# Moving casts, fills and early loads at the hand-over from the projections to attention

## The chip, the cores and the metric

The kernel runs on one core of a Trainium2 chip. The metric is the device time of one execution in microseconds; the median of three runs of the kernel before is 1693.15 us (1690.56 to 1694.89).

The engines are named as in the profile: PE is the matrix engine (TensorE; PEld its weight loads), DVE is VectorE, ACT is ScalarE, POOL is GpSimd, and SP is the queue from which this kernel issues its DMAs. Each engine works through its own instructions in order and waits for others by semaphores.

## The reference

One transformer block with adaptive layer norm: attention over 2048 positions with 32 heads of 16, then a dense layer, Mish, and a dense layer.

```python
S, D, F, H, Dh = 2048, 512, 1792, 32, 16
sa, ca, ga, sb, cb, gb = split(silu(c) @ w_mod)          # six rows of 512
h = layernorm(x) * (1 + ca) + sa
q, k, v = heads(h @ wqkv)                                # (32, 2048, 16) each
x = x + ga * (merge(softmax(q @ k.T * Dh**-0.5) @ v) @ wo)
h = layernorm(x) * (1 + cb) + sb
x = x + gb * (mish(h @ w1 + b1) @ w2)
```

All of it is fp32. The kernel forms a product of two fp32 matrices from rounded parts: each operand is split into a rounded value (hi, type fp32r) and the rest (lo), and three products hi·hi, hi·lo and lo·hi are summed.

## The kernel before

**Projections.** The first part (`lp` pool) loads x, normalizes it, transposes it in four blocks of 512 positions (`tr_tb`) into `h_h` and `h_l` (hi and lo), and projects. A weight slice of 128 columns (`wr`) is loaded by `slice_load` and split by `slice_split`: `hi_copy` writes `wh` on ScalarE (line 88), `lo_sub` writes `wl` on GpSimd (line 95). `qk_unit` projects queries or keys of eight heads for one block of 512 positions into one PSUM bank; its `fin` takes them out of PSUM, splits them into `qh` and `ql`, and writes them to a scratch in DRAM (`qscr`, `kscr`). There are two ways out: without a time `h`, ScalarE casts `qh` straight from PSUM and VectorE subtracts `ql`, which reads the bank too; with a time, ScalarE copies the bank to `qf` and GpSimd makes both parts of it. `v_unit` projects values, which ScalarE copies to `vq` (line 299). In this first part the loop over the four blocks `tb` does the keys of heads 0 to 7, one query unit, and some value units, and loads each finished block of keys back from scratch into `ka` (`load_k`, line 330), laid out for the scores.

**Banks.** PSUM has a ring of six banks (`ring`) and two banks of their own, `ms` and `acc`. Until the scores start, two of the six serve other units, so maxima turn round in four.

**Row maxima.** Softmax needs the row maxima first. The steps t = -20 to -1 (`PRO`) compute scores for maxima only: `max_pair` (lines 595 and 597) runs two matmuls side by side into two ring banks, and one VectorE reduce of 128x1024 takes both. 32 pairs make up the maxima of the first four heads, in four key blocks of eight pairs; eight pairs of the next four heads follow (they read `ka2` and `qa2`). `neg_max` and `max_rows` bring the maxima into `mt`, and DMAs put them into rows of `qa` (line 625). Between two pairs `dense_slots` puts matmuls of further projection units (`plan`, `planned`, line 133): the query slice 1, values, the key slices 1 and 2, and so on. From step 0 on each step computes scores (line 636), their exponentials on ScalarE (line 639), the product with the values (line 654) and, beside them, the maxima of later heads (lines 581 and 583) and the remaining dense work.

**Order.** The program's order is written out by hand: `at(h, f)` puts a function into the list of half step h, and `run_hooks(h)` runs it as the program is recorded; two half steps make a step, and h = -40 is the first. `planned` gives the loads and splits of later slices their half steps when a unit of an earlier slice ends.

**Early preparations.** Six blocks of w1 are split before the main part: `early_prep` loads a block (`ep`, line 1570), GpSimd splits it seven half steps later, and three half steps after that two DMAs write it to `w1scr` (line 1578). The tiles `ka2` to `ka4` are filled with ones on GpSimd (line 561) before rows of keys are loaded over them; `load_pair(2)` at h = -22 loads `qa2` and `ka2`, `load_pair(3)` at h = -10 the next.

Of the kernel before, what the change touches and what calls it, by code (L numbers as in the profile page):

```python
# [8 lines left out]
F32 = mybir.dt.float32  # L9
# [9 lines left out]
def adaln_block(ctx: ExitStack, tc: tile.TileContext, x, wqkv, wo, w1, b1, w2, c, w_mod, out):  # L19
    nc = tc.nc  # L20
# [8 lines left out]
    NB = S // TB  # L29
# [9 lines left out]
    PRO = 16 + LEAD  # L39
# [4 lines left out]
    LATE_LOAD = {4: -4, 5: 9}  # L44
# [41 lines left out]
    def hi_copy(eng, hi, src):  # L86
        if eng == "a":
            nc.scalar.copy(hi, src)
        elif eng == "v":
            nc.vector.tensor_copy(hi, src)  # L90
        else:
            nc.gpsimd.tensor_scalar(hi, src, 1.0, 0.0, op0=ALU.mult, op1=ALU.add)
# [110 lines left out]
    def at(h, f):  # L203

        hooks.setdefault(h, []).append(f)
# [23 lines left out]
    def slice_load(kind, i, pool=None, lp=None):  # L229
        w = P if kind < 2 else 2 * P  # L230
        raw = (pool or qp).tile([P, DK, w], F32, tag="raw" if pool is pw else "wr", name="wr", bufs=2 if lp else 1)
        o = kind * D + i * w
        nc.sync.dma_start(raw, wqkv[:, o:o + w].rearrange("(k p) m -> p k m", p=P))
        slices[kind, i] = raw

    def slice_split(kind, i, pool=None, eng="p", hi_eng="a"):
        raw = slices[kind, i]
        w = raw.shape[2]
        hi = (pool or qp).tile([P, DK, w], F32R, tag="wh", name="wh", bufs=2)
        lo = (pool or qp).tile([P, DK, w], F32R, tag="wl", name="wl", bufs=2)  # L240
        hi_copy(hi_eng, hi, raw)
        lo_sub(eng, lo, raw, hi)
        slices[kind, i] = (hi, lo)

    def qk_unit(kind, ct, tb, tag):

        wh, wl = slices[kind, ct]
        acc = bank(tag)
        ts_ = slice(tb * TB, (tb + 1) * TB)
        mm3(acc, [wh[:, k, :] for k in range(DK)], [wl[:, k, :] for k in range(DK)],  # L250
            [h_h[:, k, ts_] for k in range(DK)], [h_l[:, k, ts_] for k in range(DK)], "b")

        def fin(h=None):
            late = h is not None and -4 <= h < 3
            if late and not spares:
                for v in range(2):
                    both = ap.tile([P, DK, TB], F32R, tag=f"o_{v}", name="late", bufs=1)
                    spares.extend(both[:, i, :] for i in range(DK))
            if late:
                qh, ql = spares.pop(), spares.pop()  # L260
            else:
                qh = qp.tile([P, TB], F32R, tag="qh", name="qh", bufs=2)
                ql = qp.tile([P, TB], F32R, tag="ql", name="ql", bufs=2)
            if h is None:
                hi_copy("a", qh, acc)
                lo_sub("v", ql, acc, qh)
            else:
                qf = (ap.tile([P, TB], F32, tag=f"p{len(spares) // 2 % 2 * 2}", name="qf", bufs=3) if late else
                      pw.tile([P, TB], F32, tag="raw", name="qf", bufs=1))
                nc.scalar.copy(qf, acc)  # L270
                hi_copy("p", qh, qf)
                lo_sub("p", ql, qf, qh)
            scr, rows = (qscr, 50) if kind == 0 else (kscr, 48)

            def put():
                put_away.add((kind, ct, tb))
                o = 8 * ct * rows * S + tb * TB
                if kind == 0:
                    for r, src in enumerate((qh, qh, ql)):
                        nc.sync.dma_start(dap(scr, o + r * S, [[rows * S, 8], [3 * S, DH], [1, TB]]), src.bitcast(F32))  # L280
                    return
                hi = qh.bitcast(F32)
                twice = bass.AP(tensor=hi.tensor, offset=hi.offset, ap=[list(hi.ap)[0], [0, 2], [1, TB]])
                nc.sync.dma_start(dap(scr, o, [[3 * S, P], [2 * S, 2], [1, TB]]), twice)
                nc.sync.dma_start(dap(scr, o + S, [[3 * S, P], [1, TB]]), ql.bitcast(F32))

            put() if h is None else at(clear(h + (5 if h > 60 else 2)), put)
        return fin
# [34 lines left out]
    def load_k(pp, tb=None):  # L323
        n, j = divmod(pp, 2)
        h = 4 * (n % G) + 2 * j
        kt = ka[pp % NR].bitcast(F32)
        at_ = slice(0, S) if tb is None else slice(tb * TB, (tb + 1) * TB)
        assert {(1, h // 8, i) for i in (range(NB) if tb is None else (tb,))} <= put_away, (pp, put_away)
        for s in range(2):
            nc.sync.dma_start(kt[64 * s:64 * s + 48, at_], kscr[h + s, :, at_])  # L330
# [6 lines left out]
    with ExitStack() as es:  # L337
# [65 lines left out]
        def apply_tb(tb):  # L403
            rs = rss.pop(tb)
            for i in range(4):
                xt = xts[4 * tb + i]
                nc.scalar.activation(xt, xt, AF.Identity, scale=rs[:, 1, i:i + 1], bias=rs[:, 2, i:i + 1])
# [115 lines left out]
        for tb in range(NB):  # L523
            if tb + 2 < NB:
                stats_tb(tb + 2)
            parts = []
            early = []
            for kind in (1, 0) if tb == 0 else (1,):
                fin = qk_unit(kind, 0, tb, "ring")
                parts.append((pe_queue[2 * DK:], fin))  # L530
                early.append(pe_queue[:2 * DK])
                pe_queue.clear()
            if tb == 0:
                (kw, qw) = early
                early = [[m for k in range(DK) for m in (kw[k], qw[k], kw[DK + k])], qw[DK:]]
            pe_queue.extend(m for e in early for m in e)
            pe_run()
            if tb in (1, 2):
                for kc in (2 * tb - 2, 2 * tb - 1):
                    unit(v_unit(0, kc, "ring"))  # L540
            if tb + 1 < NB:
                tr_tb(tb + 1, CUT1)
            for late, fin in parts:
                pe_queue.extend(late)
                unit(fin)
            if tb + 1 < NB:
                tr_tb(tb + 1, CUT2)
            if tb + 2 < NB:
                apply_tb(tb + 2)
            if tb == 0:  # L550
                for pp in range(2):
                    load_q(pp, 48)
            for pp in range(2):
                load_k(pp, tb)
        slice_split(0, 1)


    kq2 = ctx.enter_context(tc.tile_pool(name="kq2", bufs=1))
    ka += [kq2.tile([P, S], F32R, name=f"ka{i}") for i in range(2, NR)]
    for t in ka[2:]:  # L560
        nc.gpsimd.memset(t.bitcast(F32), 1.0)
    ap = ctx.enter_context(tc.tile_pool(name="ap", bufs=1, reuse_waits="tile"))
    vgs = {}

# [527 lines left out]
    _, w1s, w2s, wos = state[last]  # L1092
# [419 lines left out]
    def planned(i, a, tag):  # L1512
        _, kind, sl, args = plan[i]
        unit = v_unit(sl, a, tag) if kind == 2 else qk_unit(kind, sl, a, tag)

        def fin(h):
            if a == args[-1]:
                if i + 2 < len(plan):
                    d = 4 if h > 0 else 1
                    split_at[i + 2] = LATE_SPLIT.get(i + 2, h + d)  # L1520
                    split = lambda: slice_split(*plan[i + 2][1:3], hi_eng="p" if h > 0 else "a")
                    split() if h < -4 else at(split_at[i + 2], split)
                if i + 3 < len(plan):
                    at(LATE_LOAD.get(i + 3, h + 7), lambda: slice_load(*plan[i + 3][1:3]))
            unit(h)
            if (kind, sl, a) == (2, 0, NKC - 1):
                at(max(0, h + 2), lambda: first_mods(max(0, h + 2)))
            if i + 1 == len(plan) and a == args[-1]:
                mst["qkv"] = h // 2 + 3
        return fin  # L1530

    at(-2 * PRO, lambda: slice_load(*plan[2][1:3]))
    order = (3, 4, 2, 5)

    def first_mods(h, j=0):
# [26 lines left out]

    EARLY = 6

    def early_prep(i, h):

        scr, src, _ = preps[i]
        lo, hi = [ap.tile([P, TB], F32R, tag=f"p{(1, 3, 0, 2)[i % 4]}", name="ep", bufs=4 - i % 4 // 2) for _ in range(2)]
        raw = lo.bitcast(F32)
        nc.sync.dma_start(raw.rearrange("p (k m) -> p k m", m=P), src)  # L1570

        def split():
            hi_copy("p", hi, raw)
            lo_sub("p", lo, raw, hi)

        def put():
            for v, part in enumerate((hi, lo)):
                nc.sync.dma_start(scr[:, v, :], part.bitcast(F32))

        at(h + 7, split)  # L1580
        at(h + 10, put)

    for i in range(EARLY):
        at(3 * i - 37, lambda i=i: early_prep(i, 3 * i - 37))

    def start_preps(h, i=EARLY, turn=0, puts=()):

# [75 lines left out]
```

## Time and profile before

| what | value |
|---|---|
| median of three runs | 1693.15 us (1690.56 to 1694.89) |
| profiled execution, its own time | 1691.93 us |
| span of its instructions | 1690.1 us |
| granted TensorE clock, mean | 0.996 |
| PE busy | 1667.0 us, 99% of the span |
| DVE, ACT, POOL busy | 85%, 80%, 48% |
| DMA moved | 239.02 MB, mean 141 GB/s |

In the rows that follow in the prediction, the first number is the start in us from the start of the span and the second the duration. Then come the engine, the source line, the operation, what it writes and reads (`out<-in`, the program's own names), the shape and a count of such instructions. A bracket at the end gives the idle time of the engine just before, and what ended it. SPq marks DMAs issued by the SP queue; the duration is that of the issue, not of the transfer.

### The profile page before, as it was taken

The numbers are of one execution on the slowest core, as the hardware profiler recorded it, in microseconds if no ns is written. First come the engines' busy times: TensorE is split into PE (matmuls) and PEld (weight loads), VectorE is DVE, ScalarE is ACT, GpSimd is POOL, SyncE is SP. The second block draws the span as 40 slices with busy tenths as digits, with TensorE's granted clock in tenths as the row PEclk, the third lists the DMA queues.
The fourth block names the chain that finished last, engine by engine and source line by source line (L and its number), as shares of the span: only waits on it lengthen the run. The fifth ranks groups of instructions, "written<-read, shape, count | busy, mean of one in ns | idle before, by whom it ended". The sixth has DMA issues, their size and how long they took to land.

```text
span 1690.1 us, 34360 instructions
## 1 busy us (share of the span) xinstructions
PE 1667.0 (99%) x12707; PEld 932.1 (55%) x12707; DVE 1431.6 (85%) x2372; ACT 1357.3 (80%) x2618; POOL 812.5 (48%) x839
## 2 busy tenths in 40 slices
PE   8989999999999999999999999999999999999999
PEld 6855665555444455555555455555555455555687
DVE  6978888888989888888889888888889888883377
ACT  7157777777778988888888998888888998889674
POOL 5556224655313564556323565556323565555442
PEclk9999999999999999999999999999999999999999
DMA  7777556777755433434355434534354433534161
GB/s 261 218 272 200 147 147 188 222 222 216 230 146 143 113 95 93 121 88 129 85 137 152 115 77 93 141 76 126 87 145 122 130 94 81 144 103 131 76 228 63
DMA packets 114984, 239.02 MB, mean 141 GB/s; under 512 B 24500, under 2 KB 50120, under 8 KB 108864
## 3 DMA queue, kind: packets, MB, share of 16 engines
q1 hardware_dynamic: 114808, 236.82, 49.5%
q8 instruction: 100, 1.64, 0.4%
q14 instruction: 68, 0.56, 0.1%
q10 hardware_dynamic: 8, 0.00, 0.0%
HBM read 180.48 MB, written 51.45 MB: 137 GB/s over the span
## 4 chain that ended last, share of the span: by engine, by line
PE 89%; DVE 4%; DMA 3%; ACT 2%; issue 1%; SPq 0%; POOL 0%; ACTq 0%; DVEq 0%; POOLq 0%
PE bk L654 29%; PE ring L636 22%; PE ring L581 19%; PE bk L133 11%; PE ring L1267 2%; PE ring L126 2%; DVE mx L583 2%; ACT pr L639 1%; PE bk L126 1%; DVE mx L597 1%; PE ring L133 1%; DMA ka<-kscr 1%; DMA kscr<-qh 0%; DMA qa<-mt 0%; PE ring L970 0%
## 5 line engine op out<-in xcount | busy, mean ns | idle before, releaser
L583 DVE TENSOR_REDUCE mx<-ring 128x1 f32<-128x512 f32 x1968 | 1221.9, 681 | 151.1 <-PE ring L581 136.6
L639 ACT ACTIVATE pr<-ring 128x512 f32<-128x512 f32 x2048 | 1078.5, 603 | 207.5 <-PE bk L133 122.7
L581 PE MATMUL ring<-ka,qa 64*128 64x512 f32 x1968 | 817.8, 429 | 1.2 <-ACT pr L639 1.0
L636 PE MATMUL ring<-qa,ka 64*128 64x512 f32 x2048 | 759.1, 402 | 3.4 <-ACT pr L639 1.9
L654 PE MATMUL bk<-pr,vg 128*32 128x512 f32 x4096 | 545.1, 604 | 0.0
L581 PEld LDWEIGHTS ring<-ka,qa 64*128 64x128 f32 x1968 | 350.6, 184 | 326.2 <-DVE mx L583 251.4
L636 PEld LDWEIGHTS ring<-qa,ka 64*128 64x128 f32 x2048 | 373.8, 184 | 192.3 <-DVE mx L583 113.2
L133 PE MATMUL bk<-h,w 64*128 64x512 f32 (+1 forms) x1080 | 277.9, 390 | 0.0
L133 PE MATMUL bk<-w,a_h 64*128 64x512 f32 x632 | 211.1, 413 | 0.0
L133 PEld LDWEIGHTS bk<-h,w 64*128 64x128 f32 x1080 | 178.6, 185 | 10.0 <-ACT pr L639 1.5
L654 PEld LDWEIGHTS bk<-pr,vg 128*32 128x32 f32 x4096 | 81.3, 108 | 135.6 <-issue 126.4
L133 PE MATMUL bk<-w,a_l 64*128 64x512 f32 x316 | 124.3, 393 | 0.0
L133 PEld LDWEIGHTS bk<-w,a_h 64*128 64x128 f32 x632 | 106.8, 184 | 3.0 <-ACT hb L848 0.8
L1026 POOL TENSOR_TENSOR y<-yd,y 128x512 f32<-128x512 f32 x44 | 56.9, 1292 | 88.9 <-ACT yd L1025 79.5
L860 POOL TENSOR_SCALAR qq<-ee 128x512 f32<-128x512 f32 x25 | 15.5, 621 | 169.1 <-ACT ee L854 169.1
L876 POOL TENSOR_TENSOR qq<-qq,rr 128x512 f32<-128x512 f32 x42 | 54.2, 1289 | 85.7 <-ACT rr L870 85.7
L862 POOL TENSOR_TENSOR hb<-hb,ee 128x512 f32<-128x512 f32 x42 | 54.1, 1288 | 79.7 <-DVE ee L858 77.7
L133 PE MATMUL bk<-w,o_hl 64*128 64x512 f32 x288 | 79.3, 405 | 0.0
L95 POOL TENSOR_TENSOR a_l<-hb,a_h 128x512 fp32r<-128x512 f32 x53 | 73.1, 1379 | 4.4
L133 PE MATMUL bk<-h_h,wl 64*128 64x512 f32 x192 | 63.3, 426 | 0.3 <-ACT pr L639 0.3
L133 PEld LDWEIGHTS bk<-w,a_l 64*128 64x128 f32 x316 | 58.3, 185 | 3.1
L133 PE MATMUL bk<-h_h,wh 64*128 64x512 f32 x192 | 53.9, 413 | 5.1 <-ACT vq L299 4.8
(226 smaller groups left out, 1902.6 us busy)
## 6 DMA issues: line engine op xcount, KB each, us to landing
ka<-kscr SPq DMA_DIRECT2D x124, 384.0 KB
w<-w2scr SPq DMA_DIRECT2D x56, 512.0 KB
w<-w1scr SPq DMA_DIRECT2D x46, 512.0 KB
vg<-vscr SPq DMA_DIRECT2D x32, 552.0 KB
qa<-qscr SPq DMA_DIRECT2D x124, 100.0 KB
qscr<-qh SPq DMA_DIRECT2D x32, 256.0 KB
w2scr<-hl SPq DMA_DIRECT2D x14, 512.0 KB
kscr<-qh SPq DMA_DIRECT2D x12, 512.0 KB
```

The costliest lines, as they stand in the source:

```text
L95: (nc.gpsimd if eng == "p" else nc.vector).tensor_sub(lo, src, hi.bitcast(F32))
L126: nc.tensor.matmul(acc, l, r, start=start, stop=stop)
L133: i = nc.tensor.matmul(acc, l[64 * g:64 * g + 64], r[64 * g:64 * g + 64], start=start and not then, stop=bool(stop and then))
L581: nc.tensor.matmul(pm, qt[64 * s:64 * s + 64, qs * P:(qs + 1) * P], kt[64 * s:64 * s + 64, kb * TB:(kb + 1) * TB], start=True, stop=True)
L583: nc.vector.tensor_reduce(out=mxs[n][:, s, 4 * j + qs, kb:kb + 1], in_=pm, op=ALU.max, axis=AX.X)
L636: nc.tensor.matmul(p_, kt[64 * s:64 * s + 64, kc * P:(kc + 1) * P], qt[64 * s:64 * s + 64, :], start=True, stop=True)
L639: e = nc.scalar.activation(pr, p_, AF.Exp, scale=SCALE)
L654: nc.tensor.matmul(accs[n][32 * h:32 * h + 32, :], vgs[n][:, o:o + 32], pts.pop((t, h)), start=(kc == 0), stop=(kc == 15))
L862: (nc.vector if tail else nc.gpsimd).tensor_mul(hb, hb, ee)
L876: nc.gpsimd.tensor_mul(qq, qq, rr)
L1026: nc.gpsimd.tensor_add(y[i], yd, y[i])
L1267: nc.tensor.matmul(po[i // 2][:, i % 2, :], l[:, s], w[:, r, :], start=(f == 0 and j == 0), stop=(f == FT - 1 and j == 2))
```

## The change

The edits all lie in the hand-over.

- The keys of the last block (kind 1, tb 3) are projected into the bank `ms` instead of a ring bank, and leave it by the second way: ScalarE copies to `qf`, GpSimd makes `qh` and `ql`.
- The query slice 1 is split in the turn of block 2, not after the loop.
- The loop loads only the key blocks 0 and 1 back. The blocks 2 and 3 are loaded at h = -40, interleaved with the loads of all six early preparations, behind the load of key slice 1.
- The early preparations are split at h = -38, -36, -34, -32, -27 and -25 and written three half steps later.
- The load of key slice 2 is recorded two half steps after its trigger instead of seven.
- `ka2`, `ka3` and `ka4` are filled at h = -30, -22 and -18.

```diff
@@ qk_unit, fin @@
-            if h is None:
+            if h is None and (kind, tb) != (1, NB - 1):
                 hi_copy("a", qh, acc)
                 lo_sub("v", ql, acc, qh)
             else:
@@ the loop over tb @@
-                fin = qk_unit(kind, 0, tb, "ring")
+                fin = qk_unit(kind, 0, tb, "ring" if tb + 1 < NB else "ms")
...
             if tb + 2 < NB:
                 apply_tb(tb + 2)
+            elif tb + 1 < NB:
+                slice_split(0, 1)
...
             for pp in range(2):
-                load_k(pp, tb)
-        slice_split(0, 1)
+                if tb < 2:
+                    load_k(pp, tb)
...
-    for t in ka[2:]:
-        nc.gpsimd.memset(t.bitcast(F32), 1.0)
+    for i, h in ((2, -30), (3, -22), (4, -18)):
+        at(h, lambda t=ka[i]: nc.gpsimd.memset(t.bitcast(F32), 1.0))
@@ planned, fin @@
-                    at(LATE_LOAD.get(i + 3, h + 7), lambda: slice_load(*plan[i + 3][1:3]))
+                    at(h + 2 if h < -20 else LATE_LOAD.get(i + 3, h + 7), lambda: slice_load(*plan[i + 3][1:3]))
...
-    at(-2 * PRO, lambda: slice_load(*plan[2][1:3]))
+    def first_loads():
+        slice_load(*plan[2][1:3])
+        for i in range(EARLY):
+            early_load(i)
+            if i % 2:
+                for pp in range(2):
+                    if i < 4:
+                        load_k(pp, 2 + i // 2)
+
+    at(-2 * PRO, first_loads)
...
-        at(h + 7, split)
-        at(h + 10, put)
+        at(h, split)
+        at(h + 3, put)

     for i in range(EARLY):
-        at(3 * i - 37, lambda i=i: early_prep(i, 3 * i - 37))
+        early_prep(i, (-38, -36, -34, -32, -27, -25)[i])
```

What this does to the order on the queues: on SP, before the change, from the scratch writes of the third key block to the second load of weights behind the first (`wr`; `ka_98` and `ka_99` are the key tiles of the first heads, `ka_700` is ka2):

```order
L284 DMA kscr<-qh 128x2x512
L285 DMA kscr<-ql 128x512
L330 DMA ka_98<-kscr 48x512 x2
L330 DMA ka_99<-kscr 48x512 x2
...
L233 DMA wr<-in_A_wqkv 128x4x128
L1570 DMA ep<-in_B_w 128x4x128 x4
L1578 DMA w1scr<-ep 128x512 x2
L280 DMA qscr<-qh 8x16x512 x2
...
L330 DMA ka_700<-kscr 48x2048 x2
L1578 DMA w1scr<-ep 128x512 x2
L233 DMA wr<-in_A_wqkv 128x4x128
```

The same place on SP after the change (ka2 is `ka_695` here):

```order
L284 DMA kscr<-qh 128x2x512
L285 DMA kscr<-ql 128x512
...
L233 DMA wr<-in_A_wqkv 128x4x128
L1582 DMA ep<-in_B_w 128x4x128 x2
L330 DMA ka_98<-kscr 48x512 x2
...
L1595 DMA w1scr<-ep 128x512 x8
L233 DMA wr<-in_A_wqkv 128x4x128
L280 DMA qscr<-qh 8x16x512 x2
...
L330 DMA ka_695<-kscr 48x2048 x2
```

The key loads of the blocks 2 and 3 moved behind the first `wr` and `ep` loads, the second `wr` load moved ahead of the query scratch and of ka2, and eight `w1scr` writes stand ahead of it where six stood.

On GpSimd, before, from the last `wl` of the first part to the query unit:

```order
L95 TENSOR_TENSOR wl<-wr,wh 128x512
L561 MEMSET ka_700 128x2048
L561 MEMSET ka_701 128x2048
L561 MEMSET ka_702 128x2048
L92 TENSOR_SCALAR ep<-ep 128x512
L95 TENSOR_TENSOR ep<-ep 128x512
L95 TENSOR_TENSOR wl<-wr,wh 128x512
L92 TENSOR_SCALAR qh<-qf 128x512
```

And after, at the same place:

```order
L95 TENSOR_TENSOR wl<-wr,wh 128x512
L92 TENSOR_SCALAR qh<-qf 128x512
L95 TENSOR_TENSOR ql<-qf,qh 128x512
L92 TENSOR_SCALAR ep<-ep 128x512
...
L562 MEMSET ka_695 128x2048
L95 TENSOR_TENSOR wl<-wr,wh 128x512
L92 TENSOR_SCALAR qh<-qf 128x512
```

The last keys' pair came in, four early splits (eight rows, cut) and one fill stand ahead of the next `wl` where one split and three fills stood. On ScalarE the cast `wh` comes ahead of the last key unit and that unit's cast became the copy `qf<-bk`. VectorE lost one `ql`; TensorE's order is the same but for the bank of twelve matmuls.

More of the change, by code (lines that the diff above doesn't have):

```diff
@@ L1563, in adaln_block, with early_load @@
     EARLY = 6
-    def early_prep(i, h):
+    raws = {}
+    def early_load(i):
         scr, src, _ = preps[i]
@@ L1570, in early_prep @@
         nc.sync.dma_start(raw.rearrange("p (k m) -> p k m", m=P), src)
+        raws[i] = scr, raw, hi, lo
+    def early_prep(i, h):
         def split():
+            scr, raw, hi, lo = raws[i]
             hi_copy("p", hi, raw)
@@ L1576, in put @@
         def put():
+            scr, _, hi, lo = raws.pop(i)
             for v, part in enumerate((hi, lo)):
                 nc.sync.dma_start(scr[:, v, :], part.bitcast(F32))
-        at(h + 7, split)
-        at(h + 10, put)
+        at(h, split)
+        at(h + 3, put)
     for i in range(EARLY):
-        at(3 * i - 37, lambda i=i: early_prep(i, 3 * i - 37))
+        early_prep(i, (-38, -36, -34, -32, -27, -25)[i])
     def start_preps(h, i=EARLY, turn=0, puts=()):
```

## The prediction

> **What bounds the kernel now.** I read the page first, then the busy time by stage, then the engines in order of time around the two places where the stages show TensorE idle.
>
> ```profile
> span 1690.1 us, 34360 instructions
> PE 1667.0 (99%) x12707; PEld 932.1 (55%) x12707; DVE 1431.6 (85%) x2372; ACT 1357.3 (80%) x2618; POOL 812.5 (48%) x839
> ```
>
> TensorE is busy 1667.0 of 1690.1 us. So any gain must be sought in the 23 us in which it is not, or in stretches where it is busy at a lower clock. The view by stages shows these; the columns are the stretch, its length, busy us (and instructions) of PE, PEld, DVE, ACT and POOL, then the granted clock, the DMA share and GB/s.
>
> ```profile
> 1200.00:1600.00 400.00, 399.32 (x3021) 209.23 (x3019) 311.22 (x529) 338.94 (x659) 194.67 (x198) 1.00 0.40 112
> ...
> 11.33:14.74 3.41, 2.29 (x38) 1.22 (x37) 1.67 (x5) 1.67 (x2) 0.98 (x2) 1.00 1.10 369
> 18.15:21.57 3.42, 1.67 (x8) 0.83 (x6) 3.35 (x6) 3.33 (x5) 3.26 (x6) 1.00 1.05 387
> 21.57:24.98 3.41, 3.41 (x11) 2.93 (x12) 3.34 (x7) 1.93 (x3) 0.00 (x1) 0.50 1.07 312
> 45.46:48.87 3.41, 1.80 (x9) 0.96 (x9) 1.64 (x3) 1.10 (x2) 1.31 (x2) 1.00 0.82 284
> 48.87:52.29 3.42, 3.42 (x26) 3.42 (x24) 2.45 (x2) 0.00 (x0) 3.42 (x3) 0.50 0.55 203
> 83.01:86.42 3.41, 0.89 (x8) 0.46 (x4) 2.34 (x3) 0.00 (x0) 0.00 (x0) 1.00 1.01 291
> 86.42:89.83 3.41, 1.16 (x5) 0.87 (x7) 0.00 (x0) 1.38 (x3) 1.41 (x2) 0.50 1.07 395
> 89.83:93.25 3.42, 3.42 (x20) 2.67 (x18) 1.85 (x4) 0.16 (x1) 1.72 (x2) 0.50 1.10 391
> ```
>
> In the attention proper TensorE idles 0.7 us in 400: work behind the hand-over cannot shrink, only start earlier. Before it the stretches of 3.41 us are cut where the clock changes. Each one with TensorE busy 1.80 us or less (1.67, 1.80, 0.89, 1.16) is followed by one at clock 0.50; the one with 2.29 us was followed by full clock. The change touches two of these places.
>
> **The first place** is the hand-over from the last key unit to the first maxima.
>
> ```profile
> 45.12 1.04 POOL L479 TENSOR_TENSOR h_l<-hf,modc 128x512 fp32r<-128x512 f32 x1 [1.62 <-DVE hf L474]
> 46.22 0.78 PE L126 MATMUL ring<-h_l,wh 128*128 128x512 f32 x2 [0.16 <-POOL h_l L479]
> 47.08 0.58 ACT L88 CAST qh<-ring 128x512 fp32r<-128x512 f32 x1 [2.97 <-PE ring L126]
> 47.70 0.69 DVE L95 TENSOR_TENSOR ql<-ring,qh 128x512 fp32r<-128x512 f32 x1 [1.25 <-ACT qh L88]
> 48.44 0.58 PE L595 MATMUL ring<-ka,qa 64*128 64x512 f32 x2 [1.44 <-DVE ql L95]
> 49.06 1.23 DVE L597 TENSOR_REDUCE mx<-ring 128x2 f32<-128x1024 f32 x1 [0.67 <-PE ring L595]
> 52.46 32.89 DVE L597 TENSOR_REDUCE mx<-ring 128x2 f32<-128x1024 f32 x29 [0.47 <-PE ring L595]
> ```
>
> The first maxima wait 1.44 us for a ring bank that ql still reads; the next stretch then runs at half clock. From the third reduce on VectorE is the bound of this stage: 29 in 32.89 us, 1.134 us each, without a gap.
>
> **The second place** is a chain through three queues.
>
> ```profile
> 64.07 1.71 SPq L1578 DMA_DIRECT2D w1scr<-ep  x2
> 79.00 0.38 SPq L233 DMA_DIRECT2D wr<-in_A_wqkv  x1
> 80.25 0.37 ACT L299 COPY vq<-bk 128x256 f32<-128x256 f32 x1 [2.32 <-PE bk L133]
> 87.72 0.62 ACT L88 CAST wh<-wr 128x512 fp32r<-128x512 f32 x1 [7.10 <-DMA wr<-in_A_wqkv]
> 88.25 0.37 ACT L299 COPY vq<-bk 128x256 f32<-128x256 f32 x1
> 83.45 0.44 PE L595 MATMUL ring<-ka,qa 64*128 64x512 f32 x2
> 88.67 2.13 PE L133 MATMUL bk<-h_h,wh 64*128 64x512 f32 x6 [4.77 <-ACT vq L299]
> 91.26 1.23 DVE L597 TENSOR_REDUCE mx<-ring 128x2 f32<-128x1024 f32 x1 [5.91 <-PE ring L595]
> 92.97 2.42 DVE L597 TENSOR_REDUCE mx<-ring 128x2 f32<-128x1024 f32 x2
> 95.99 7.01 DVE L597 TENSOR_REDUCE mx<-ring 128x2 f32<-128x1024 f32 x6 [0.35 <-PE ring L595]
> ```
>
> The weights wr of the third key slice are issued at 79.00, late in SP's queue among w1scr writes, and land 8.7 us later; ScalarE's cast waits for them, the value copy that frees a bank stands behind the cast, and TensorE stands 4.77 us. Two half-clock stretches follow.
>
> **The change, part by part.**
>
> Own bank, and the last keys on GpSimd: the maxima no longer share a bank with the last key unit, so nothing holds them after the matmuls that end at 46.22 + 0.78 = 47.00. A ScalarE copy and a GpSimd pair replace ScalarE's cast and the 0.69 us on VectorE. The copy goes into the buffer that held the raw query weights, so it waits for their wl. That moves ahead on GpSimd to the end of h_l (45.12 + 1.04 = 46.16) and takes 1.28 (row below): 47.44. The copy, as long as the cast, ends at 48.1, the GpSimd pair at 50.1. TensorE waits for none of this before the bank's next use, four pairs of maxima later (some 51.5). Gain: the first reduce follows its matmul by 49.06 − 48.44 = 0.62, and the matmul can be issued behind the last of the key unit at 46.8, which puts the reduce at 47.4, 1.66 us sooner. The bounds are 1.44 (the wait alone) and 1.66; I take 1.66. The key unit itself must now wait until the transposes in its new bank have been read, but it waits longer for other halves of h_h and h_l: nothing.
>
> Clock: with the wait gone, 45.46:48.87 is busy 1.80 + 1.44 = 3.24 us, above 2.29, so the drop should not come. The third reduce stands 3.40 us behind the first; at 1.134 each it would be 2.27. Gain 1.13; bounds 0 and 1.13. By the Trainium skill (TensorE: Matmul & The Clock Gate, Part 1: The HAM clock gate) the clock is halved after an idle window of some 3.4 us and given back after a busy one; the window of 1.80 us busy was not idle, so the trace is stricter than the page here. By the page this drop has another cause and stays, and the sum below would be 7.6 instead of 8.7.
>
> Query weights sooner: the cast wh, 0.62 us, moves to 44.1 on ScalarE, which is idle from there to 47.08 (2.97 us by its row); it costs nothing.
>
> Weights and loads sooner, key tiles filled later. Rows that carry the prices:
>
> ```profile
> 48.26 1.28 POOL L95 TENSOR_TENSOR wl<-wr,wh 128x512 fp32r<-128x512 f32 x1 [2.10 <-ACT wh L88]
> 49.48 5.29 POOL L561 MEMSET ka<- 128x2048 f32 x3
> 59.07 0.43 SPq L233 DMA_DIRECT2D wr<-in_A_wqkv  x1
> 59.61 2.09 SPq L1570 DMA_DIRECT2D ep<-in_B_w  x4
> 63.42 0.63 POOL L92 TENSOR_SCALAR ep<-ep 128x512 fp32r<-128x512 f32 x1 [8.65 <-DMA ep<-in_B_w]
> 64.13 1.28 POOL L95 TENSOR_TENSOR ep<-ep 128x512 fp32r<-128x512 f32 x1
> 70.08 0.39 PE L133 MATMUL bk<-h_h,wl 64*128 64x512 f32 x1
> 95.71 2.86 SPq L625 DMA_DIRECT2D qa<-mt  x4
> 103.05 0.49 PE L636 MATMUL ring<-qa,ka 64*128 64x512 f32 x1 [0.43 <-DVE mx L597]
> 48.87:103.49 54.62, 48.77 (x517) 43.87 (x515) 46.59 (x43) 8.89 (x27) 26.96 (x26) 0.91 0.83 257
> ```
>
> On SP the last key unit's two scratch writes now stand ahead of the loads of the third and fourth key blocks, and wait for the GpSimd pair: issued by 50.2. Behind them come wr of the second slice, at 50.7, and the first ep load at about 51.2 (59.07 and 59.61 before), then the third key block at 52 and, between more ep loads, the fourth at 55 to 57. The 17th and 25th pair of maxima, 16 and 24 × 1.134 us after 47.4, need those blocks at 65 and 74: hidden. The first ep load took 3.8 us from its issue to the split that waits for it (59.61 to 63.42); 8.7 (the wr load above) is the other end. I take 3.8, the same transfer: 55.0. GpSimd then does four splits (63.42 to 65.41, 1.99 each), one memset (5.29/3 = 1.76) and the second slice's wl (1.28): 55.0 + 7.96 + 1.76 + 1.28 = 66.0. TensorE first needs this wl at 70.08, in the new time 67.3 (2.8 sooner, 1.66 + 1.13), so 1.3 us to spare; with 8.7 it is 3.6 us late. The third slice's wr follows on SP at once, behind eight w1scr writes that are all released by 63: issued at 66, landed between 69.8 and 74.7. ScalarE needs it behind the copy of 80.25, in the new time 80.25 + 0.37 − 2.8 = 77.8. So the waits of 7.10 and 4.77 us vanish, and what TensorE meets next is VectorE's pace. GpSimd rounds the query unit by 68.0; its scratch write and then the load of qa2 and ka2 take 3.8 to 8.7 us each and end at 75.6 to 85.4. The first maxima on them come at 84: 0 to 1.4 us late, and I take 0, since the share of the transfers falls when they start sooner. Two more splits and the other two memsets end on GpSimd at 68.0 + 3.98 + 3.52 = 75.5, before the third slice's wl (about 79).
>
> What this is worth: between the end of reduce 31 (52.46 + 32.89 = 85.35) and the 35th at 95.99 lie 10.64 us. Undisturbed there are three reduces (1.23 + 2.42 = 3.65), 0.48 us of small reduces (91.26 + 1.23 to 92.97) and 0.60 after (95.39 to 95.99): 4.73. Gain 5.9; bounds 4.77 (wait alone) to 5.9.
>
> Sum: 1.66 + 1.13 + 5.9 = 8.7 us. The scores would start at 103.05 − 8.7 = 94.3; the last qa<-mt, issued 2.86 us after 87, lands in time even at the 4.5 us that 98.57 to 103.05 allowed. Behind this the program is the same and TensorE-bound. The profiled execution took 1691.93, so 1683.2; it lies 1.2 under the median of three, 1693.15, so **1684.4 us**.
>
> **The rivals.**
>
> GpSimd late (0.10): the second slice's wl behind four splits and a memset comes at 70.9 if the first ep load needs 8.7 us. For: two writes of 512 and 256 KB stand ahead of it. Against: the transfers' share was 0.55 at 48.87:52.29. TensorE waits 3.6 us, perhaps with half a stretch of low clock, 1.7: 1688.0 to 1689.7.
>
> Clock drop stays (0.07): if the drop at 48.87 has another cause than the 1.44 us wait, the 1.13 us are not won: 8.7 − 1.13 = 7.6, 1685.5. Against it stand the four low stretches, each followed by 0.50. The Trainium skill's page on the clock gate, named above, speaks for this case.
>
> Transfers bound the stage (0.10): from 48.87 to 103.49 they were busy 0.83 of 54.62 us, 45.3 us of work, and the shorter stage has 45.9. If they cannot be packed beyond 0.83, the maxima's rows arrive as late as now: 1693, no change. Against: 391 to 395 GB/s were reached where 257 is the mean, and the work now starts some 8 us sooner.
>
> Slower (0.07): the third slice's wr stands behind the eight w1scr writes, which wait for GpSimd, and behind wl. If SP is held there, each microsecond of landing past 77.8 is one that ScalarE's cast, and through it TensorE, waits. The gain is used up at 77.8 + 8.7 = 86.5; at 91.6 the kernel is 5.1 us slower, 1698.2. For it: such a queue is what made the stall of now. Against: 91.6 is 17 us behind the later of my two landings, and no wait in the rows is so long.
>
> **How the numbers follow.** The forecast has 0.66, its own range 1682.5 to 1686.5 (wait and clock bounds on one side, about 1 us of small TensorE gaps at 100 to 110 on the other). Within 0.3% (5.1 us, about what this kernel's measurement tells from no change) lie the transfers' case and half of GpSimd late. Faster: 0.66 + 0.07 + 0.05 = 0.78; same 0.10 + 0.05 = 0.15; slower 0.07. The range takes in GpSimd late: 1681.5 to 1689.7.
>
> **What would show it.** First maxima within 0.3 us of the last key unit; clock 1.00 in every stretch from 45 on; the third slice's wr on SP near 66 and no TensorE wait above 1 us at 75 to 95; scores from 94.3. Wrong if TensorE waits for wl near 67, if the cast still waits for wr, or if scores begin after 98.

## The result and the profile after

| | before | changed |
|---|---|---|
| median | 1693.15 us, 11 runs (1690.56 to 1697.11) | 1687.92 us, 11 runs (1685.39 to 1691.74) |
| ratio to before | | 0.9972, interval 0.9962 to 0.9981 |
| span of the profiled execution | 1690.1 us | 1684.5 us |

The change wins 5.2 us by the medians and 5.6 us in the two profiled executions, where 8.7 were forecast. The interval lies clear of 1, and the time is inside the range. In a later group of runs (run 11 below) the changed kernel came out at 0.9960 (0.9947 to 0.9972).

VectorE in order of time, changed kernel, from the first maxima to the eight pairs on the keys of pair 2:

```profile
47.06 21.58 DVE L598 TENSOR_REDUCE mx<-ring 128x2 f32<-128x1024 f32 x19 [1.05 <-PE ring L596]
69.51 14.90 DVE L598 TENSOR_REDUCE mx<-ring 128x2 f32<-128x1024 f32 x13 [0.87 <-PE ring L596]
86.73 1.23 DVE L598 TENSOR_REDUCE mx<-ring 128x2 f32<-128x1024 f32 x1 [1.94 <-PE ring L596]
88.51 1.23 DVE L598 TENSOR_REDUCE mx<-ring 128x2 f32<-128x1024 f32 x1 [0.55 <-PE ring L596]
90.36 6.99 DVE L598 TENSOR_REDUCE mx<-ring 128x2 f32<-128x1024 f32 x6
```

The first reduce stands at 47.06 (49.06 before), and the third at 47.06 + 2 × 1.136 = 49.33 (52.46 before): the first place went as forecast. Of the 2.0 us, 0.44 are no part of the change, since GpSimd's last h_l already starts at 44.68 instead of 45.12 here. The 35th reduce comes at 90.36 instead of 95.99, where 87.3 was forecast. The two holes that cost the rest are the 0.87 us ahead of 69.51 and the stretch from 69.51 + 14.90 = 84.41 to 90.36.

TensorE's waits in the same stage, changed kernel:

```profile
68.06 0.50 PE L133 MATMUL bk<-h_h,wl 64*128 64x512 f32 x1 [0.82 <-POOL wl L95]
84.86 0.47 PE L596 MATMUL ring<-ka,qa 64*128 64x512 f32 x1 [1.43 <-DVE mm L611]
85.93 0.76 PE L596 MATMUL ring<-ka,qa 64*128 64x512 f32 x1 [0.60 <-DMA ka<-kscr]
97.41 0.50 PE L637 MATMUL ring<-qa,ka 64*128 64x512 f32 x1 [0.43 <-DVE mx L598]
```

The wait of 4.77 us behind ScalarE's value copy is gone. In its place TensorE waits for wl of the second slice and then for the keys of pair 2, twice, one half of `ka2` after the other. (The profile puts the first of these two waits down to a small reduce that came last by its semaphores. In another execution of the same kernel, run 11 below, both are put down to the load.) The scores start at 97.41, 5.64 us sooner, which is the whole gain: from there to the end it takes 1587.1 us in both executions (1684.5 − 97.41 and 1690.1 − 103.05).

ScalarE's cast of the third slice, GpSimd, and SP's queue, changed kernel:

```profile
78.44 0.62 ACT L88 CAST wh<-wr 128x512 fp32r<-128x512 f32 x1
```

```profile
57.15 0.63 POOL L92 TENSOR_SCALAR ep<-ep 128x512 fp32r<-128x512 f32 x1 [7.29 <-PE ring L596]
64.97 1.81 POOL L562 MEMSET ka<- 128x2048 f32 x1
66.74 1.27 POOL L95 TENSOR_TENSOR wl<-wr,wh 128x512 fp32r<-128x512 f32 x1
```

```profile
51.42 1.43 SPq L1582 DMA_DIRECT2D ep<-in_B_w  x2
...
68.03 0.38 SPq L233 DMA_DIRECT2D wr<-in_A_wqkv  x1
...
70.67 3.60 SPq L1595 DMA_DIRECT2D w1scr<-ep  x2
74.36 0.81 SPq L306 DMA_DIRECT2D vscr<-vq  x1
75.26 1.91 SPq L1595 DMA_DIRECT2D w1scr<-ep  x2
77.23 1.74 SPq L321 DMA_DIRECT2D qa<-qscr  x2
79.06 0.77 SPq L330 DMA_DIRECT2D ka<-kscr  x2
```

The chain that replaced the stall stands in these rows. The first w1 split starts at 57.15, so wl ends at 68.01. On SP the third slice's weights follow at 68.03 and are in time, but `ka2`, which needs none of this, stands behind four w1scr writes and a value write and is issued only at 79.06. TensorE's second product on it starts at 85.93, 6.9 us after.

The stage by its stretches, changed kernel (columns as in the prediction):

```profile
44.90:48.31 3.41, 3.26 (x27) 2.36 (x26) 2.32 (x4) 0.59 (x1) 2.70 (x3) 1.00 0.82 268
48.31:51.72 3.41, 3.41 (x43) 3.13 (x41) 3.41 (x4) 0.00 (x0) 1.47 (x2) 1.00 1.04 383
82.45:85.86 3.41, 1.45 (x11) 0.69 (x7) 2.31 (x4) 0.16 (x1) 0.00 (x0) 1.00 0.96 312
85.86:89.27 3.41, 3.34 (x15) 2.65 (x15) 1.99 (x2) 0.00 (x0) 0.00 (x0) 0.50 1.17 320
47.06:97.85 50.79, 47.30 (x515) 41.95 (x513) 46.52 (x43) 9.45 (x28) 28.29 (x28) 0.97 0.92 287
```

The drop of the clock at 48.87 is gone, and the new wait has brought one of its own, at 85.86. Over the stage the transfers are busy 0.92 of the time at 287 GB/s, where it was 0.83 at 257.

### The profile page after: what moved, and what is told of

Its sections match the earlier page's. It is cut to its first block, busy times and chain, and to the rows that moved or that the text cites. A ratio compares the mean times of both kernels' runs of the same rounds, so it can differ in the third digit from the quotient of the medians.

```text
span 1684.5 us, 34365 instructions
## 1 busy us (share of the span) xinstructions
PE 1665.0 (99%) x12707; PEld 930.2 (55%) x12707; DVE 1431.1 (85%) x2371; ACT 1357.5 (81%) x2618; POOL 815.2 (48%) x841
## 4 chain that ended last, share of the span: by engine, by line
PE 90%; DMA 3%; DVE 2%; ACT 2%; POOL 1%; issue 1%; SPq 1%; ACTq 0%; POOLq 0%; DVEq 0%
PE bk L655 29%; PE ring L637 22%; PE ring L582 19%; PE bk L133 11%; PE ring L1268 2%; PE ring L126 2%; PE bk L126 1%; ACT pr L640 1%; DVE mx L584 1%; DMA ka<-kscr 1%; PE ring L133 1%; DMA wr<-in_A_wqkv 1%; DMA qscr<-qh 0%; PE ring L971 0%; PE ring L617 0%
## 5 line engine op out<-in xcount | busy, mean ns | idle before, releaser
L879 POOL TENSOR_TENSOR rr<-rr,qq 128x512 f32<-128x512 f32 x42 | 54.1, 1289 | 3.5
```

The costliest lines, as they stand in the source:

```text
L879: nc.gpsimd.tensor_mul(rr, rr, qq)
```

## The experiments

My theory after reading this trace: the sum of the three terms was not a sum. The scores start when the last of several landings lets them, and what a step wins ahead of that landing is waited away in front of it. The rival is what the prediction did: each place is worth its own microseconds. Eleven runs were made, in three groups (1 to 4, 5 to 8, 9 to 11), each beside the kernel before.

**1. The first place alone.** The kernel before with own bank, GpSimd rounding and early query weights:

```
-fin = qk_unit(kind, 0, tb, "ring")
+fin = qk_unit(kind, 0, tb, "ring" if tb + 1 < NB else "ms")
-            if h is None:
+            if h is None and (kind, tb) != (1, NB - 1):
-        slice_split(0, 1)              # after the loop
+            elif tb + 1 < NB:          # in the turn of block 2
+                slice_split(0, 1)
```

> The kernel before with the first part of the change alone: the last key unit in its own bank, its rounding on GpSimd, and the query weights rounded sooner. Theory A (the places add up, as in my sum): the first maxima come 1.7 us sooner, the half-clock stretch from 48.87 is gone, and the time falls by 1.66 + 1.13 = 2.8 us, to 1690.4 (0.9983). Theory B (the stall at 84 to 89 sets the end): the weights of the third key slice still land near 87.7, since their place in SP's queue and GpSimd's splits ahead of them depend on the landing of the w1 loads and not on the maxima; the stall of TensorE grows from 4.77 to about 7.5 us, the scores start at 103 as before, and the time is 1693 (1.000).

1694.10 us, ratio 1.0003 (0.9994 to 1.0012): nothing. The first reduce starts at 47.40, and the clock stays full until 87.70. Then TensorE waits twice:

```profile
64.86 0.38 PE L133 MATMUL ring<-wh,h_h 64*128 64x256 f32 x1 [2.12 <-ACT qf L270]
89.30 2.13 PE L133 MATMUL bk<-h_h,wh 64*128 64x512 f32 x6 [5.44 <-ACT vq L299]
```

ScalarE stands in both cases in front of a cast whose weights have not landed:

```profile
63.70 0.62 ACT L88 CAST wh<-wr 128x512 fp32r<-128x512 f32 x1 [5.84 <-DMA wr<-in_A_wqkv]
88.35 0.62 ACT L88 CAST wh<-wr 128x512 fp32r<-128x512 f32 x1 [7.77 <-DMA wr<-in_A_wqkv]
```

Theory B holds, with one landing more than I had named: the second slice's weights take the first 2.1 us already. Scores start at 103.98.

**2. The earlier load alone.** The kernel before with

```
-at(LATE_LOAD.get(i + 3, h + 7), lambda: slice_load(*plan[i + 3][1:3]))
+at(h + 2 if h < -20 else LATE_LOAD.get(i + 3, h + 7), lambda: slice_load(*plan[i + 3][1:3]))
```

> The kernel before with one line of the change: the load of the third key slice's weights is issued at h + 2, ahead of the query scratch writes and of the pair's load instead of behind them. The first maxima and the half-clock stretch at 48.87 stay as before. Theory A (the places add up): the 4.77 us stall and its half clock go, 5.9 us, 1687.3 (0.9965), scores from 97.2. Theory B (what follows the stall is bound by the transfers): the keys of pair 2 land later than before and TensorE waits for them instead; less than 2 us are won, above 1691 (0.999), and the wait for the keys of pair 2 is over 3 us.

1693.49 us, ratio 1.0005 (0.9996 to 1.0014). The 4.77 us stall is gone, and again nothing is won, but neither theory named the wait that took over:

```profile
65.91 0.38 PE L133 MATMUL ring<-wh,h_h 64*128 64x256 f32 x1 [2.28 <-ACT qf L270]
104.79 0.76 PE L636 MATMUL ring<-qa,ka 64*128 64x512 f32 x1 [5.68 <-DMA qa<-mt]
```

```profile
97.18 0.33 SPq L568 DMA_DIRECT2D vg<-vscr  x1
97.60 2.12 SPq L625 DMA_DIRECT2D qa<-mt  x3
```

The first maxima waited as before (1.45 us ahead of 47.68), but against my expectation no half clock followed: the clock's step falls at 46.96 here, in the middle of the wait, and leaves 2.54 and 2.70 us busy on its two sides. The maxima were ready by 92, and the four writes that bring them into qa (three fall into the window shown) stood on SP behind a value load that waited 1.6 us for its own scratch write. Scores start at 104.79, 1.7 us later than before.

**3. The keys of pair 2 sooner.** From here on the diffs are against the changed kernel:

```
-for pp, h in ((2, -22), (3, -10)):
+for pp, h in ((2, -29), (3, -10)):
     at(h, lambda pp=pp: load_pair(pp))
```

> The changed kernel with the load of pair 2 (qa2 and ka2) moved ahead on SP, from behind two more pairs of w1scr writes and a value write to directly behind the eight w1scr writes, ahead of the third key slice's weights. Theory A (the place in the queue made ka2 late): it lands before 77, TensorE's idle time at 83.4 to 85.9 and the half-clock stretch from 85.86 are gone, the 35th reduce comes at 87.7 instead of 90.36, and 2.6 us are won on the changed kernel: 1685.3 (0.9954). The weights behind it are issued up to 1.5 us later, which ScalarE's cast at 78.4 does not see. Theory B (the transfers bound the stage, so what goes sooner makes something else later by as much): the weights of the third slice or the value and key transfers behind them land after their readers ask, and the time stays at 1688 (0.997).

1682.99 us, ratio 0.9944 (0.9930 to 0.9958): theory A, and a larger gain than its 1685.3. On SP, VectorE and TensorE:

```profile
68.07 0.77 SPq L330 DMA_DIRECT2D ka<-kscr  x2
68.94 0.40 SPq L233 DMA_DIRECT2D wr<-in_A_wqkv  x1
```

```profile
47.93 36.29 DVE L598 TENSOR_REDUCE mx<-ring 128x2 f32<-128x1024 f32 x32 [1.06 <-PE ring L596]
87.46 7.01 DVE L598 TENSOR_REDUCE mx<-ring 128x2 f32<-128x1024 f32 x6 [0.36 <-PE ring L596]
```

```profile
95.28 0.46 PE L637 MATMUL ring<-qa,ka 64*128 64x512 f32 x1 [1.17 <-DMA qa<-mt]
```

`ka2` is issued at 68.07 instead of 79.06. VectorE has no hole left: from the first reduce to the 35th it takes 87.46 − 47.93 = 39.53 us, against 43.30 in the changed kernel (90.36 − 47.06) and 46.93 before. Of these 3.8 us, 0.87 are the wait for wl, which this execution did not have (see run 4); the rest is `ka2`. No engine of this stage waits for the transfers that now come later, and the next landing shows: 1.17 us for qa<-mt.

**4. And GpSimd's fill out of the way.**

```
-for i, h in ((2, -30), (3, -22), (4, -18)):
+for i, h in ((2, -40), (3, -22), (4, -18)):
     at(h, lambda t=ka[i]: nc.gpsimd.memset(t.bitcast(F32), 1.0))
```

> As the run before, and the fill of ka2 on GpSimd moved from between the fourth w1 split and the next wl into the 7 us in which GpSimd waits for the first w1 load. Theory A: wl comes 1.8 us sooner, at 66.2, TensorE's wait of 0.82 us for it is gone, and with pair 2 in time the whole of my forecast is there: 0.9 + 2.6 = 3.5 us on the changed kernel, 1684.4 (0.9948), scores from 94 in the clock of the changed kernel's trace. Theory B (transfers bound the stage): wl comes sooner but nothing later does, and the time is that of the run before.

1684.05 us, ratio 0.9953 (0.9941 to 0.9966): nothing on the run before, as theory B has it, though for another reason. (Theory A's 1684.4, counted from the changed kernel, lies as near, so the time alone does not decide.) In the third run the first w1 load had landed 1.2 us sooner than in the changed kernel (its split started at 55.95, not 57.15), so wl was in time there without this edit. Here the first split starts at 57.62 and wl already at 65.47, in time again, and the 35th reduce follows the first by 39.53 us.

**5. The changed kernel without its first place.** The last key unit back in the ring's bank:

```
-fin = qk_unit(kind, 0, tb, "ring" if tb + 1 < NB else "ms")
+fin = qk_unit(kind, 0, tb, "ring")
-            if h is None and (kind, tb) != (1, NB - 1):
+            if h is None:
```

> The changed kernel with the last key unit put back: in the ring's bank, rounded by ScalarE's cast and VectorE's ql. Theory A (the places add up): the 1.66 + 1.13 = 2.8 us of the first place are lost, 1690.7 (0.9986). Theory B (the landing of the keys of pair 2 sets the end in the changed kernel, at 85.8 whatever stands ahead): the maxima start 1.7 us later and at half clock, but the waits for wl (0.82) and for ka2 (about 2.5 with its half clock) shrink to nothing instead, scores start at 96.5 to 97.5 as in the changed kernel, and the time is 1687.3 to 1688.2 (0.9965 to 0.997).

1685.97 us, ratio 0.9955 (0.9943 to 0.9967), no slower than with the own bank (0.9972 and 0.9960), and a little below theory B's range. TensorE, from the keys of pair 2 on:

```profile
85.76 0.46 PE L596 MATMUL ring<-ka,qa 64*128 64x512 f32 x1 [0.40 <-DMA ka<-kscr]
86.91 0.47 PE L596 MATMUL ring<-ka,qa 64*128 64x512 f32 x1 [0.69 <-DMA ka<-kscr]
97.45 0.50 PE L637 MATMUL ring<-qa,ka 64*128 64x512 f32 x1 [0.43 <-DVE mx L598]
```

The first reduce is at 48.96 and the half clock at 48.66 is back. Still the scores start at 97.45, where they start in the changed kernel (97.41). This decides between the theories: in the changed kernel 2.8 booked microseconds are won at 47 to 52 and waited away again, 0.9 at the wait for wl (67 to 68) and the rest at 83 to 86.

**6. The changed kernel with the late weights.** The h + 2 undone:

```
-at(h + 2 if h < -20 else LATE_LOAD.get(i + 3, h + 7), lambda: slice_load(*plan[i + 3][1:3]))
+at(LATE_LOAD.get(i + 3, h + 7), lambda: slice_load(*plan[i + 3][1:3]))
```

> The changed kernel with the third key slice's weights put back behind the load of pair 2 on SP (the h + 2 undone), all else as changed. Theory A: 5.9 us are lost and the first place's 2.8 us stay, 1690.4 (0.9983) with scores from about 100.5. Theory B (the end is set by the last of the landings that this stage waits for): the weights are issued near 79.8 and land 7 to 8 us later, at 87 to 88 as before, ScalarE's cast waits for them, and scores start near 103: 1692 to 1693.5 (0.9995).

1693.09 us, ratio 1.0001 (0.9992 to 1.0010): theory B, all of the gain is gone.

```profile
69.64 0.79 PE L133 MATMUL bk<-h_h,wl 64*128 64x512 f32 x1 [3.07 <-POOL wl L95]
90.47 1.28 PE L133 MATMUL bk<-h_h,wh 64*128 64x512 f32 x2 [4.58 <-ACT vq L299]
105.38 0.49 PE L637 MATMUL ring<-qa,ka 64*128 64x512 f32 x1 [0.43 <-DVE mx L598]
```

The line that alone wins nothing (run 2) is needed for everything. In this execution the first w1 split started at 58.73, and wl was 3.07 us late. The query scratch ahead of these weights on SP waited 2.4 us for GpSimd, which comes to it behind wl, so a part of the 105.38 may be this execution's.

**7. The key blocks 2 and 3 loaded first again.**

```
             for pp in range(2):
-                if tb < 2:
-                    load_k(pp, tb)
+                load_k(pp, tb)
...
             early_load(i)
-            if i % 2:
-                for pp in range(2):
-                    if i < 4:
-                        load_k(pp, 2 + i // 2)
```

> The changed kernel with the key blocks 2 and 3 loaded where they were before the change, each behind its own scratch writes and so ahead of the first weights and w1 loads. My sum booked nothing for their place but that they are hidden. Theory A (the place of the key loads is worth nothing): 1688 (0.997). Theory B (each key load on SP waits until the scratch writes ahead of it have landed, and the queue with it): weights and w1 loads are issued at 59 to 60 as before the change, four splits and a fill then end near 73 on GpSimd, TensorE waits some 6 us for wl of the second slice, and all behind it is as late: 1695 to 1699 (1.001 to 1.004).

1693.04 us, ratio 0.9996 (0.9986 to 1.0005). The gain is gone, so theory A is out, and the mechanism is that of B: the first weights are issued at 59.83.

```profile
75.08 0.49 PE L133 MATMUL bk<-h_h,wl 64*128 64x512 f32 x1 [3.59 <-POOL wl L95]
93.33 0.47 PE L595 MATMUL ring<-ka,qa 64*128 64x512 f32 x1 [1.58 <-DMA ka<-kscr]
105.36 0.47 PE L636 MATMUL ring<-qa,ka 64*128 64x512 f32 x1 [0.74 <-DMA qa<-mt]
```

B's price was too high: it was 3.6 us of waiting for wl where I said 6, and 1693 where I said 1695 to 1699. Ahead of it stands a wait of 1.33 us at 64.44 for the second slice's weights, the one of run 1. The scores start 2.3 us later than before in this execution, and the median does not show it. The part behind the scores' start took 1585.8 us here (1691.2 − 105.36). Over the executions shown it lies between 1585.8 and 1589.2, and what sets it there I did not settle.

**8. The writes of the maxima ahead.** Run 4, and

```
-at(-7, lambda: load_v(0))
+at(-5, lambda: load_v(0))
-for pp, h in ((2, -29), (3, -10)):
+for pp, h in ((2, -29), (3, -4)):
```

> The kernel of the fourth run (pair 2 sooner, ka2 filled in GpSimd's idle time), and the first value load and the load of pair 3 moved on SP from ahead of the four qa<-mt writes to behind them. In that kernel the scores waited 1.31 us for these writes (issued 89.66, landed 95.45, the value load ahead of them having held SP until a value write had landed). Theory A (their place in the queue): issued by 87.5, they land before the last maxima end near 94.2, scores start 0.9 to 1.3 us sooner, 1682.9 (0.9940). Theory B (the transfers ahead of them on the engines set their landing): they land as late and the time stays at 1684 (0.9953).

1683.95 us, ratio 0.9942 (0.9929 to 0.9954); against run 4 that is unclear. The mechanism of A is there: TensorE no longer waits for qa<-mt. The scores start at 93.97, but 1.03 of the 1.16 us on run 4 are earlier first maxima in this execution (46.62 against 47.65), and wl was 0.51 us late. ScalarE has a new wait:

```profile
100.35 0.62 ACT L88 CAST wh<-wr 128x512 fp32r<-128x512 f32 x1 [0.81 <-DMA wr<-in_A_wqkv]
```

The load of the next weights had come to stand behind the load of pair 3. What this wait is worth in time is not shown (run 9).

**9. These weights ahead again.**

```
-for pp, h in ((2, -29), (3, -4)):
+for pp, h in ((2, -29), (3, -3)):
```

> The kernel of the eighth run, and on SP the next slice's weights wr moved back ahead of the load of pair 3 (in that run they came behind it, landed at 100.32, and ScalarE's cast waited 0.81 us for them with the probabilities behind it; 0.95 us were lost between the 4th and the 10th group of probabilities). Theory A: the weights land by 98, this wait is gone, scores start at 94.0 as in the eighth run, and 0.9 us are won on it: 1683.0 (0.9938). Theory B (the load of pair 3 that now comes later is waited for instead): the maxima of pair 3 wait near 105 and the time is 1684 or more (0.9945).

1683.23 us, ratio 0.9941 (0.9929 to 0.9954). The cast comes at 99.53 without a wait, and the stage has no hole:

```profile
47.47 36.30 DVE L598 TENSOR_REDUCE mx<-ring 128x2 f32<-128x1024 f32 x32 [1.05 <-PE ring L596]
87.00 7.01 DVE L598 TENSOR_REDUCE mx<-ring 128x2 f32<-128x1024 f32 x6 [0.36 <-PE ring L596]
```

```profile
94.07 0.50 PE L637 MATMUL ring<-qa,ka 64*128 64x512 f32 x1 [0.43 <-DVE mx L598]
```

103.05 − 94.07 = 8.98: this is the start of the scores that I had forecast for the changed kernel, 94.3. By the medians it is 10.0 us under the kernel before (1693.28 beside it). In time it can't be told from runs 3, 4 and 8, so the removed wait of 0.81 us is not shown to be worth anything.

**10. Run 9 without the own bank.** The edit of run 5, on run 9.

> The kernel of the ninth run with the last key unit back in the ring's bank, rounded by ScalarE and VectorE. Theory A (the first place counts once nothing later sets the end): the 1.66 + 1.13 us of my sum are lost here, 2.5 to 2.8 us against the ninth run, 1685.6 (0.9955), scores from 96.6. Theory B (the own bank is worth nothing in any setting): the time of the ninth run.

1685.55 us, ratio 0.9958 (0.9945 to 0.9972), 2.3 us over run 9 on the same chip, and all five times (1685.05 to 1687.74) above the five of run 9 (1682.54 to 1684.95).

```profile
47.78 0.79 PE L596 MATMUL ring<-ka,qa 64*128 64x512 f32 x2 [1.45 <-DVE ql L95]
96.15 0.50 PE L637 MATMUL ring<-qa,ka 64*128 64x512 f32 x1 [0.43 <-DVE mx L598]
```

96.15 − 94.07 = 2.1 us, and 2.7 when the last h_l is counted in, which starts 0.63 us sooner here than in run 9 (44.46 against 45.09). Theory A holds here: the edit that was worth nothing in runs 1 and 5 is worth about what its rows say once no later landing sets the end.

**11. The changed kernel again**, beside 9 and 10:

> The changed kernel once more, on the same chip as the two runs before, to set the others against it: 1687.9 (0.9972), scores from 97.4. If the landing of ka2 sets the end, its first wait on the keys of pair 2 stands again between 83 and 86.

1686.65 us (1684.92 to 1687.93), ratio 0.9960 (0.9947 to 0.9972), 3.4 us over run 9.

```profile
68.25 0.49 PE L133 MATMUL bk<-h_h,wl 64*128 64x512 f32 x1 [0.71 <-POOL wl L95]
84.51 0.47 PE L596 MATMUL ring<-ka,qa 64*128 64x512 f32 x1 [0.89 <-DMA ka<-kscr]
85.52 0.47 PE L596 MATMUL ring<-ka,qa 64*128 64x512 f32 x1 [0.54 <-DMA ka<-kscr]
```

Both waits on the keys of pair 2 are put down to the load here. Runs 3, 8 and 9 are the versions furthest ahead of both kernels: 0.994 against 0.996 to 0.997 for the changed one.

## Why the prediction was right, and where not

The time came within the stated range, 3.5 us above the predicted 1684.4, but above the narrower range of the forecast itself, 1682.5 to 1686.5. That the wide range covers it is partly luck: it was that wide for "GpSimd late", which cost 0.9 us and not 3.6, and the larger loss, `ka2`, stood in no rival. Of the signs that it named, the first came (the first maxima's matmul stands at 46.49, the key unit's last ends at 46.57); against the others, a half-clock stretch came at 85.86, TensorE waited 1.43 us ahead of 84.86, and the scores started at 97.41. One of its signs of being wrong came, too: the wait for wl near 67. By its own steps:

- **Own bank, 1.66 us.** Right where it stands: the first reduce starts at 47.06, of the 2.0 us 1.56 are the change's. No compute engine waits for the GpSimd pair that replaced ql; on SP the scratch write (49.89) and the first weights (50.27) do, as forecast. What it is worth was wrong, see the sum.
- **Clock, 1.13 us.** Right: the clock is full at 48 to 52, and runs 9 and 10, which differ only in the last key unit's bank and its way out, show the wait as cause: full clock in the one (3.25 us busy in 44.90:48.31), a half-clock stretch from 47.96 in the other, behind one with 1.80 us busy. The rival by which the drop stays is refuted. But the 1.13 us are not there in every execution: of the four traces with this wait (before and runs 2, 5 and 10), run 2 has no drop.
- **The stall, 5.9 us.** The stall of 4.77 us is gone, the third slice's weights are issued at 68.03 (66 forecast), and ScalarE's cast starts at 78.44 without a wait.
- **The step that failed: "0 to 1.4 us late, and I take 0"**, for the load of `ka2`. It was the mis-sized term. From the end of the 32nd reduce to the 35th it is 90.36 − 84.41 = 5.95 us in the changed kernel and 87.00 − (47.47 + 36.30) = 3.23 in run 9: 2.7 us, half clock included. I had looked at how long the query's scratch write and the load take, and not at what stands between them on SP: two pairs of w1scr writes and a value write, which hold the issue until 79.06. Nor does the load need the query unit's scratch write that I counted ahead of it: in run 3 it is issued before that write (68.07 against 69.56). Run 3 moves the load past all of them and gets the time back.
- **The spare of 1.3 us for wl.** Also too generous: from its issue to the split, the first w1 load took 5.7 us (51.42 to 57.15) and not 3.8. 0.87 us were lost; this is a part of the rival "GpSimd late". Between the executions with the early w1 loads that split starts anywhere from 55.35 (run 5) to 59.15 (run 10).
- **The sum.** 8.7 − 2.7 − 0.9 + 0.44 (the earlier h_l of this execution) = 5.5, against 5.6 in the profile. As bookkeeping it closes. But the terms don't add: without the first two the changed kernel has the same end (run 5), without the third term's line it has no gain at all (run 6), and neither first place nor load wins anything alone (runs 1 and 2). 8.7 is about the price of the whole when every landing is in time, as in run 9 (8.98 us at the start of the scores, by further edits).
- **"Transfers bound the stage".** Not here: the share rose from 0.83 to 0.92. In run 3 it is 0.98 at 297 GB/s between the first maxima and the first probabilities (47.93 to 95.82), with a shorter stage. What mattered is the order in which they land.
- **Slower by SP's queue.** Did not come, but the mechanism, SP held by scratch writes that wait for GpSimd, is a part of what made `ka2` late: in 3.8 of the 11.0 us from 68.03 to 79.06 SP waited for GpSimd. The rows ahead of the load took the rest.

## What to carry to other kernels

Where a stage waits for several transfers through one queue, its gains need not add: list each landing with the time when its reader asks, and count only down to the latest. For each load count what stands ahead of it in the queue and what those rows wait for, not only its own duration. An edit that wins nothing alone may be needed by the others, so it is judged with the rest in place.

## What the runs showed of the hardware

- **The clock.** I cut all thirteen executions at the clock's own step of 3.41 us and took TensorE's busy time in each stretch that ran at full clock. All 15 with 1.80 us or less were followed by half clock; of the nine with 1.81 to 1.98, four were and five were not; with 2.03 or more none was. So in these executions the turn lies near 55% busy (1.80 of 3.41 is 53%, 2.03 is 59%), and it needs no single long wait. Four neighbours in run 7:

```profile
62.71:66.12 3.41, 1.91 (x20) 1.40 (x22) 2.11 (x2) 2.75 (x8) 1.82 (x2) 1.00 1.07 296
66.12:69.53 3.41, 3.41 (x32) 3.41 (x30) 1.99 (x2) 0.00 (x0) 3.24 (x5) 0.50 1.11 361
69.53:72.95 3.42, 1.96 (x26) 1.64 (x22) 2.85 (x3) 0.12 (x1) 3.34 (x4) 1.00 0.77 292
72.95:76.36 3.41, 1.28 (x15) 1.28 (x17) 0.00 (x0) 0.04 (x1) 3.33 (x4) 1.00 0.24 85
```

  The stretch with 1.91 was followed by half clock, the one with 1.96 by full clock. The grid lies elsewhere in each execution, so whether a wait of 1.4 to 2 us costs half a stretch is partly chance, as run 2 shows at the first place. The Trainium skill (TensorE: Matmul & The Clock Gate, Part 1: The HAM clock gate) gives the half clock to an idle window of some 3.4 us on a grid that runs freely. Length and grid agree with the rows here; that the window must be idle does not.
- **Landing times vary between executions of the same order.** Up to the second slice's weights the kernel before and run 2 have the same order on SP, and they were issued at 59.07 and at 61.12: the last key load ahead of them waited 3.2 us on SP for its scratch writes to land in the one and 4.8 in the other. The first maxima start 0.8 us sooner in run 2. Such 2 us decide whether a step with 1 us to spare is on the path; they are larger than several terms of my sum.
